# Writing out every engine's order by hand in a recurrent-attention and expert kernel

## The chip, the cores and the metric

The kernel runs on one core of a Trainium2 chip. The metric is the device time of one execution in microseconds (us), lower is better. TensorE (PE) multiplies matrices, VectorE (DVE), ScalarE (ACT) and GpSimd (POOL) work elementwise, and SyncE (SP) issues the DMA transfers. Each engine works through its own list of instructions in the order in which the program lays it down, and instructions of different engines wait for each other by semaphores.

## The reference

Two stages follow each other. The first is a linear attention with decay, over 4 batches, 8 heads, 768 steps and a head size of 48; the second is a dense layer pair with an unusual activation on the resulting 3072 tokens of width 384.

```python
for t in range(S):
    kt, vt, rt = (k[:, :, t], v[:, :, t], r[:, :, t])
    cur = np.einsum('bhd,bhe->bhde', u[None] * kt, vt)
    y[:, :, t] = np.einsum('bhd,bhde->bhe', rt, state + cur)
    state = w[None, :, :, None] * state + np.einsum('bhd,bhe->bhde', kt, vt)
# x: y as 3072 tokens x 384
h = x @ w_in                       # 384 -> 2048
sp = np.maximum(h, 0.0) + np.log1p(np.exp(-np.abs(h)))
g = h * erf(sp)
return (g @ w_out).astype(np.float32)   # 2048 -> 384
```

All of it is float32. w lies between 0.85 and 0.95.

## The kernel before

**Attention.** The 768 steps are cut into chunks of 128; with 4 batches there are 24 chunks g, four of which (one of each batch) make one block of 512 tokens. Within a chunk the recurrence becomes matrix products, for which r and k are scaled by powers of w. A chunk passes through named steps: L loads it, K and R scale k and r (L180, L184, 112 x 512 each), N scales the k that lies the other way round (L188, 128 x 384), Q forms the diagonal: two multiplies (L200, L201), a sum (L202) and two spread-out halves `am` (L211 on ScalarE as four small multiplies, or L213 on GpSimd as one large). A is the product of k and r on TensorE (L232), whose masked part is copied over `am` (L239); Y multiplies by v and adds the part of the carried state `sbd` (L256); S forms the state's increment `ds` (L279) and updates `sbd` (L289 to L292); X splits the result into a high and a low half (L301, L302), for the next stage.

**Expert layers.** Float32 accuracy comes from pairs of numbers: each operand is a high half that TensorE takes at full rate and the remainder, and three products stand for one. A step n is one block b of 512 tokens and one of 16 slices f of the 2048 columns, 96 steps in all; the first two blocks are worked through in halves of eight slices, with partial sums kept in DRAM. `f1` makes h with nine matmuls (L319). The activation is a chain of ScalarE and VectorE instructions of 128 x 512: two tanh (L326, L327), a combination (L329), tanh and two squares (L335 to L337), a product with h (L342), the high half `gh` (L348) and the remainder `gl` (L354, on VectorE or GpSimd). `f2` adds nine matmuls into three accumulators (L371). There are three buffers for h, two for each tile of the chain.

**Weights.** They come as 64-bit words, in 16 groups of 768 columns, and are turned into the high and low halves on the chip: L114 (ScalarE), L115, L116, L118 (VectorE), L120 (ScalarE, the high half) and L121 (VectorE or GpSimd, the low half). Group 0 of `win` is needed for f 0 and 1, and so on; all 16 groups are turned while the first two blocks run.

**Order.** A table `PLAN` gives each step of a chunk and of a weight group a place on the scale of the step number n, `FFN` gives the distances of the pieces of one step, and the program emits all pieces sorted by that place. The framework's own scheduler then orders the instructions anew within each engine, from its estimates of their durations. Three tables, `ONDVE`, `ONACT` and `GLP`, and `SUBDVE` for the weights, say which engine takes which elementwise piece. TensorE is given some matmuls on zeros (`keep_warm`, L85) where it would stand idle early on.

```python
for n in range(NS):
    for d, f in zip(FFN, (f1, act_a, act_b, act_c, act_d, act_e, f2)):
        todo.append((n + d - (0.95 if f is f1 and n == NS - 1 else 0), f, (n,)))
for (what, *args), pos in PLAN.items():
    todo.append((pos, parts[what], args[:1] if what == "W" else args))
todo.sort(key=lambda x: x[0])
```

A second path under `tc.If` serves values of w that the fast path can't take; it doesn't run with these inputs.

Of the kernel before, what the change touches and what calls it, by code (L numbers as in the profile page):

```python
# [9 lines left out]
F32 = mybir.dt.float32  # L10
# [30 lines left out]
def body(ctx: ExitStack, tc: tile.TileContext, att, wcol, u, win, wout, levels, outT):  # L41
# [20 lines left out]
    def load_chunk(g, parts=((0, V0), (V0, AW))):  # L62
        if g >= NCH:
            return
        if g not in chunks:
            chunks[g] = (xp if g == 3 else apool).tile([P, AW], F32, tag="x" if g == 3 else "att", name=f"att{g}")
        for c0, c1 in parts:
            nc.sync.dma_start(out=chunks[g][:, c0:c1], in_=att[g, :, c0:c1])
# [33 lines left out]
    def load_w(which, g):
        if (which, g) not in raws:
            fetch_w(which, g)
        raw = raws.pop((which, g))
# [4 lines left out]
        words = raw.bitcast(I32).rearrange("p (n two) -> p n two", two=2)  # L110
        wl, wh = words[:, :, 0], words[:, :, 1]
        t = stage.tile([P, WG], I32, tag="wt", name=f"wt{which}{g}", bufs=WTB)
        v = t.bitcast(F32)
        nc.scalar.activation(out=v, in_=wh.bitcast(F32), func=AF.Copy, scale=2.0 ** -112)  # L114
        nc.vector.tensor_scalar(out=t, in0=t, scalar1=3, scalar2=None, op0=ALU.logical_shift_left)  # L115
        nc.vector.scalar_tensor_tensor(out=t, in0=wl, scalar=29, in1=t,  # L116
                                       op0=ALU.logical_shift_right, op1=ALU.bitwise_or)
        nc.vector.scalar_tensor_tensor(out=t, in0=wh, scalar=-0x80000000, in1=t,  # L118
                                       op0=ALU.bitwise_and, op1=ALU.bitwise_or)
        nc.scalar.copy(out=hi, in_=v)  # L120
        (nc.vector if (which, g) in SUBDVE else nc.gpsimd).tensor_tensor(out=lo, in0=v, in1=hi.bitcast(F32), op=ALU.subtract)  # L121
# [56 lines left out]
    def prep_k(g):  # L178
        t = chunks[g][:PR, 512:V0]
        pick("k", g).tensor_tensor(out=t, in0=t, in1=wk.rearrange("p a c -> p (a c)"), op=ALU.mult)  # L180

    def prep_r(g):
        t = chunks[g][:PR, 0:512]
        pick("r", g).tensor_tensor(out=t, in0=t, in1=wr.rearrange("p a c -> p (a c)"), op=ALU.mult)  # L184

    def prep_n(g):
        t = chunks[g][:, K0:R0]
        pick("n", g).tensor_tensor(out=t, in0=t, in1=wknf, op=ALU.mult)  # L188

    def prep_q(g):  # L190
        st_[g] = dict(t=chunks[g], am=diagonal(chunks[g], g))

    def pick(what, g):
        return nc.vector if what in ONDVE.get(g, "") else nc.gpsimd

    def diagonal(t, g):

        q = a2.tile([P, NPAIR, 2], F32, tag="q", name=f"q{g}")
        kn, rn = t[:, K0:R0], t[:, R0:AW]
        pick("q", g).tensor_tensor(out=rn, in0=rn, in1=ub, op=ALU.mult)  # L200
        pick("q", g).tensor_tensor(out=rn, in0=rn, in1=kn, op=ALU.mult)  # L201
# [16 lines left out]
    def a_step(g):  # L218
# [15 lines left out]
        for hh in range(2):  # L234
            predicated(s["am"][hh], ap[hh], mask.bitcast(U32), hh)
# [356 lines left out]
```

## Time and profile before

| | |
|---|---|
| time, median of 3 runs | 572.49 us (570.76 to 576.68) |
| time of the profiled execution | 572.33 us |
| its span, first to last instruction | 570.2 us |
| busy: PE, DVE, ACT, POOL | 536.0, 338.7, 392.2, 268.7 us |
| mean granted TensorE clock | 0.968 |

In the rows below, a group reads: line, engine, operation, output <- inputs, shapes, count | busy us, mean ns of one | idle time just before them and who ended it. In a timeline the first number is the start in us, the second the length. A digit of the slices is the busy share in tenths of one fortieth of the span. Matmuls are pipelined, so the lengths of neighbours overlap; from one start to the next is the better measure.

### The profile page before, as it was taken

What the parts mean: (1) busy time and instruction counts of PE and PEld (TensorE: products, weight loads), DVE (VectorE), ACT (ScalarE), POOL (GpSimd) and SP (SyncE); (2) the same over time, 40 slices, a digit from 0 to 9 for tenths busy, and PEclk for the clock granted to TensorE, in tenths of its full rate; (3) what the DMA queues carried; (4) which work ended last, traced back from release to release, by engine and by line L of the source; (5) the groups of instructions that cost most, each with busy time, mean ns of one, the idle gap of its engine ahead of it and who ended that gap; (6) DMA issues with size and microseconds to landing.
All of it is one profiled execution on the core that took longest, in us unless ns stands there. A gap on an engine that the chain in (4) does not pass through costs nothing.

```text
span 570.2 us, 10334 instructions
## 1 busy us (share of the span) xinstructions
PE 536.0 (94%) x4107; PEld 405.1 (71%) x4107; DVE 338.7 (59%) x533; ACT 392.2 (69%) x701; POOL 268.7 (47%) x242
## 2 busy tenths in 40 slices
PE   7848988898999999999999999999999999999994
PEld 3526766675766777777777777777777778888882
DVE  8798877988657576573744345546642333445342
ACT  2424836568998946776768784776696668888783
POOL 6994489984363366474473128835412412000000
PEclk9776997999999999999999999999999999999999
DMA  7652434344243052233220014202210000010002
GB/s 290 241 214 77 172 138 143 130 137 167 64 142 109 1 174 101 82 119 118 82 83 0 2 57 162 81 1 82 82 56 1 2 1 1 0 57 0 1 0 60
DMA packets 20773, 48.89 MB, mean 86 GB/s; under 512 B 1648, under 2 KB 10992, under 8 KB 20720
## 3 DMA queue, kind: packets, MB, share of 16 engines
q1 hardware_dynamic: 20720, 48.18, 25.0%
q8 instruction: 34, 0.56, 0.4%
q14 instruction: 19, 0.16, 0.1%
HBM read 41.88 MB, written 6.29 MB: 84 GB/s over the span
## 4 chain that ended last, share of the span: by engine, by line
PE 69%; DVE 13%; ACT 6%; POOL 4%; issue 3%; DMA 2%; DVEq 0%; POOLq 0%; ACTq 0%
PE h L319 30%; PE acc L371 29%; PE y L256 5%; PE A L232 4%; DVE wt L118 2%; DVE wt L116 1%; DVE gl L354 1%; PE ds L279 1%; DVE s L329 1%; DVE s L342 1%; DVE wt L115 1%; DVE am L239 1%; ACT gh L348 1%; POOL am L213 1%; ACT wt L114 1%
## 5 line engine op out<-in xcount | busy, mean ns | idle before, releaser
L319 PE MATMUL h<-x,wih 128*128 128x512 f32 x576 | 191.8, 410 | 8.1 <-DVE s L342 4.4
L354 POOL TENSOR_TENSOR gl<-s,gh 128x512 fp32r<-128x512 f32 x49 | 64.2, 1313 | 155.8 <-ACT gh L348 150.3
L319 PEld LDWEIGHTS h<-x,wih 128*128 128x128 f32 x576 | 108.2, 193 | 39.0 <-DVE s L342 6.9
L319 PE MATMUL h<-x,wil 128*128 128x512 f32 x288 | 116.8, 406 | 0.0
L371 PE MATMUL acc<-gl,woh 128*128 128x512 f32 x288 | 115.5, 401 | 1.4 <-POOL gl L354 0.9
L342 DVE SCALAR_TENSOR_TENSOR s<-s,h 128x512 f32<-128x512 f32 x96 | 65.7, 685 | 83.1 <-ACT s L337 82.7
L371 PE MATMUL acc<-gh,wol 128*128 128x512 f32 x288 | 113.7, 395 | 0.0
L329 DVE SCALAR_TENSOR_TENSOR s<-s,h 128x512 f32<-128x512 f32 x96 | 65.7, 684 | 62.2 <-ACT s L327 52.5
L371 PE MATMUL acc<-gh,woh 128*128 128x512 f32 x288 | 96.6, 403 | 0.5 <-ACT gh L348 0.5
L335 ACT ACTIVATE s<-s 128x512 f32<-128x512 f32 x96 | 60.4, 629 | 48.0 <-DVE s L329 47.9
L348 ACT CAST gh<-s 128x512 fp32r<-128x512 f32 x96 | 59.0, 615 | 33.3 <-DVE s L342 26.0
L326 ACT ACTIVATE s<-h 128x512 f32<-128x512 f32 x96 | 57.1, 595 | 31.1 <-PE h L319 30.1
L319 PEld LDWEIGHTS h<-x,wil 128*128 128x128 f32 x288 | 55.3, 192 | 14.6 <-issue 0.8
L371 PEld LDWEIGHTS acc<-gl,woh 128*128 128x128 f32 x288 | 54.1, 188 | 16.1 <-issue 1.6
L371 PEld LDWEIGHTS acc<-gh,woh 128*128 128x128 f32 x288 | 53.3, 188 | 16.2 <-issue 2.2
L371 PEld LDWEIGHTS acc<-gh,wol 128*128 128x128 f32 x288 | 54.1, 188 | 12.0
L336 ACT ACTIVATE s<-s 128x512 f32<-128x512 f32 x96 | 60.4, 629 | 1.8
L337 ACT ACTIVATE s<-s 128x512 f32<-128x512 f32 x96 | 60.3, 629 | 1.5
L327 ACT ACTIVATE s<-s 128x512 f32<-128x512 f32 x96 | 60.3, 628 | 1.3
L213 POOL TENSOR_TENSOR am<-ident,q 128x512 f32<-128x512 f32 x37 | 43.0, 1182 | 38.5 <-PE y L256 30.8
L354 DVE TENSOR_TENSOR gl<-s,gh 128x512 fp32r<-128x512 f32 x47 | 40.1, 856 | 18.9 <-ACT gh L348 18.1
L239 DVE COPY_PREDICATED am<-mask,A 64x256 f32<-64x256 uint32 x96 | 40.1, 443 | 17.3 <-PE A L232 13.5
(72 smaller groups left out, 579.8 us busy)
## 6 DMA issues: line engine op xcount, KB each, us to landing
att<-in_att_dram SPq DMA_DIRECT2D x24, 608.0 KB, 5.0
att<-in_att_dram SPq DMA_DIRECT2D x24, 512.0 KB, 3.7
raw<-in_win_dram SPq DMA_DIRECT2D x8, 768.0 KB, 4.3
raw<-in_wout_dram SPq DMA_DIRECT2D x8, 768.0 KB, 4.4
out_dram<-o SPq DMA_DIRECT2D x18, 256.0 KB, 2.6
part<-o SPq DMA_DIRECT2D x6, 256.0 KB, 3.7
o<-part SPq DMA_DIRECT2D x6, 256.0 KB, 2.8
ub<-in_u_dram SPq DMA_DIRECT2D x1, 192.0 KB, 6.0
```

The source lines that it names most:

```text
L213: nc.gpsimd.tensor_tensor(out=m, in0=ident[:, hh:hh + 1].to_broadcast([P, NPAIR, C]), in1=q[:, :, hh:hh + 1].to_broadcast([P, NPAIR, C]), ...
L319: nc.tensor.matmul(out=h, lhsT=w[:, f, q, :], rhs=x[:, xi, q, :], start=k == 0, stop=k == 8)
L326: nc.scalar.activation(out=s1, in_=e["h"], func=AF.Tanh, bias=FB0, scale=FA0)
L327: nc.scalar.activation(out=s1, in_=s1, func=AF.Tanh, bias=FB1, scale=FA1)
L329: nc.vector.scalar_tensor_tensor(out=s2, in0=s1, scalar=FG, in1=e["h"], op0=ALU.mult, op1=ALU.add)
L335: nc.scalar.activation(out=s, in_=s, func=AF.Tanh, bias=FB2, scale=FA2)
L336: nc.scalar.activation(out=s, in_=s, func=AF.Square, bias=FB3, scale=FA3)
L337: nc.scalar.activation(out=s, in_=s, func=AF.Square, bias=FB4, scale=FA4)
L342: nc.vector.scalar_tensor_tensor(out=g, in0=g, scalar=FC, in1=e["h"], op0=ALU.subtract, op1=ALU.mult, reverse0=True)
L348: nc.scalar.copy(out=gh, in_=e["g"])
L354: (nc.gpsimd if GLPOOL(n) else nc.vector).tensor_tensor(out=gl, in0=e["g"], in1=e["gh"].bitcast(F32), op=ALU.subtract)
L371: nc.tensor.matmul(out=acc[e], lhsT=w[:, f, es], rhs=g, start=first and i == 0, stop=last and i == 2)
```

## The change

`PLAN`, `FFN` and the four tables of engines are gone. In their place stands one string, `ORDER`, of 1710 words, each one instruction or one block of instructions; the program emits them in just this sequence, inside `tc.manual_schedule()`, so that each engine's list is the sequence of its words. For that the steps are cut finer: the activation into a, b, z, c, d, e, g, h, l, the weights into C..a to C..f, the diagonal into Qa, Qb, Qc and M, the masked copies into P, the state into D and Sa to Sd, the split into Xa and Xb, the loads into their two halves, the outputs into Oa to Oc. f is `f1`, p is `f2`. A "+" at the end of a word puts it on GpSimd, a "*" on ScalarE, else VectorE or the engine that the step always has. The arithmetic of a step is as before.

| elementwise pieces on GpSimd | before | after |
|---|---|---|
| K, R (112 x 512) | 17, 18 of 24 | 8, 8 |
| N, Qa, Qb (128 x 384) | 20, 23, 23 of 24 | 5, 10, 7 |
| halves of `am` | 37 of 48 | 17 (17 on ScalarE, 14 on VectorE) |
| state times w^128 | 32 of 32 | 21 |
| low halves of the weights | 9 of 16 | 5 |
| `gl` | 49 of 96 | 43 |

`keep_warm` asks for 84 matmuls on zeros in all (16 ahead of the words, 68 by words), 37 before.

```diff
+    fixed = ctx.enter_context(ExitStack())
+    fixed.enter_context(tc.manual_schedule())
...
-    load_chunk(0, ((0, V0),))
-    load_chunk(1, ((0, V0),))
     ub = const.tile([P, 384], F32, name="ub")
-    nc.sync.dma_start(out=ub, in_=u.partition_broadcast(P))
+
+    def load_u():
+        nc.sync.dma_start(out=ub, in_=u.partition_broadcast(P))
...
+    def load_w(part, eng, which, g):
...
+        if part == "a":
+            nc.scalar.activation(out=v, in_=wh.bitcast(F32), func=AF.Copy, scale=2.0 ** -112)
+        elif part == "b":
+            nc.vector.tensor_scalar(out=t, in0=t, scalar1=3, scalar2=None, op0=ALU.logical_shift_left)
...
+        else:
+            eng.tensor_tensor(out=lo, in0=v, in1=hi.bitcast(F32), op=ALU.subtract)
...
+    def prep_k(g, eng):
         t = chunks[g][:PR, 512:V0]
-        pick("k", g).tensor_tensor(out=t, in0=t, in1=wk.rearrange("p a c -> p (a c)"), op=ALU.mult)
+        eng.tensor_tensor(out=t, in0=t, in1=wk.rearrange("p a c -> p (a c)"), op=ALU.mult)
...
+    def diag_m(q, g, hh, eng):
...
+        if eng is nc.scalar:
+            for p in range(NPAIR):
+                nc.scalar.mul(out=m[:, p, :], in_=ident[:, hh], mul=q[:, p, hh:hh + 1])
+        else:
+            eng.tensor_tensor(out=m, in0=ident[:, hh:hh + 1].to_broadcast([P, NPAIR, C]),
+                              in1=q[:, :, hh:hh + 1].to_broadcast([P, NPAIR, C]), op=ALU.mult)
...
-    for n in range(NS):
-        for d, f in zip(FFN, (f1, act_a, act_b, act_c, act_d, act_e, f2)):
-
-            todo.append((n + d - (0.95 if f is f1 and n == NS - 1 else 0), f, (n,)))
...
+    words = ORDER.split()
+    last = max(i for i, x in enumerate(words) if x[0] == "C")
+    for i, x in enumerate(words):
+        eng = {"+": nc.gpsimd, "*": nc.scalar}.get(x[-1], nc.vector)
+        what, x = x[0], x.rstrip("+*")
+        num = int("".join(c for c in x if c.isdigit()))
+        sub = x[-1]
+        if what == "l":
+            act_l(num, eng)
+        elif what in steps:
+            steps[what](num)
...
+    fixed.close()
...
-WARM = (21, 4)
...
+WARM = 16
 WG, RAWB, WTB = 768, 2, 1
...
+ORDER = """
+U0 L0a L0b L1a L1b Q0a+ L2a K0 L3a T0 R0 Q0b A0 F00 Q1a Q0c R1+ M01* F10 M00 N0 P00 R2+ W8 D0 P01 L2b C00a K2+ S0a W3
+Y0 S0b L3b Q1b A2 X0a K1 N1 A1 L4a Q1c K3+ X0b M10* D1 L4b S1b Q2a+ S1a M11* P10 Q3a+ P11 Q2b+ W10 Y1 K4 Q4a X1a L5a
...
+O230b h25 O230c l25+ f24 O232b O232c f26 a24 O231a b24 z24 c24 D9 f27 a26 S9a L11a S9b S9c+ d24 O231b b26 S9d L14a e24
...
+p71 d73 c74 e73 d74 g73 Y21 a75 e74 b75 g74 p72 X21a X21b Y22 h74 h73 l74+ f77 X22a l73 X22b z75 p73 c75 a77 d75 b77
...
+O950a O950b O951a O952a O951b O952b
+"""
```

More of the change, by code (lines that the diff above doesn't have):

```diff
@@ L98, in fetch_w @@
     def fetch_w(which, g):
-        raw = raws[which, g] = stage.tile([P, WG], I64, tag="raw", name=f"raw{which}{g}")
+        raws[which, g] = raw = stage.tile([P, WG], I64, tag="raw", name=f"raw{which}{g}")
         nc.sync.dma_start(out=raw, in_=(wout if which else win)[:, g * WG:(g + 1) * WG])
[L102 to L105, printed above, removed]
+    bits = {}
+    def load_w(part, eng, which, g):
+        words = raws[which, g].bitcast(I32).rearrange("p (n two) -> p n two", two=2)
+        wl, wh = words[:, :, 0], words[:, :, 1]
+        if part == "a":
+            bits[which, g] = stage.tile([P, WG], I32, tag="wt", name=f"wt{which}{g}", bufs=WTB)
+        t = bits[which, g]
+        v = t.bitcast(F32)
         hi, lo = (woh, wol) if which else (wih, wil)
@@ L109, in load_w @@
         hi, lo = hi.rearrange(pat)[:, s], lo.rearrange(pat)[:, s]
[L110 to L121, printed above, removed]
+        if part == "a":
+            nc.scalar.activation(out=v, in_=wh.bitcast(F32), func=AF.Copy, scale=2.0 ** -112)
+        elif part == "b":
+            nc.vector.tensor_scalar(out=t, in0=t, scalar1=3, scalar2=None, op0=ALU.logical_shift_left)
+        elif part == "c":
+            nc.vector.scalar_tensor_tensor(out=t, in0=wl, scalar=29, in1=t,
+                                           op0=ALU.logical_shift_right, op1=ALU.bitwise_or)
+        elif part == "d":
+            nc.vector.scalar_tensor_tensor(out=t, in0=wh, scalar=-0x80000000, in1=t,
+                                           op0=ALU.bitwise_and, op1=ALU.bitwise_or)
+        elif part == "e":
+            nc.scalar.copy(out=hi, in_=v)
+        else:
+            eng.tensor_tensor(out=lo, in0=v, in1=hi.bitcast(F32), op=ALU.subtract)
     ident = const.tile([P, 2, P], F32, name="ident")
@@ L372, in f2, with put_out, end @@
                                  start=first and i == 0, stop=last and i == 2)
-        if not last:
-            return
-        for e in range(NQ):
-            o = fp.tile([P, TB], F32, tag="s1" if n == NS - 1 and e == 2 else "o", name=f"o{n}_{e}")
-            if f < NF - 1:
-                nc.scalar.copy(out=o, in_=acc[e])
-                pt = part[b, e] = dp.tile([P, TB], F32, tag=f"part{b}{e}", name=f"part{b}{e}")
-                nc.sync.dma_start(out=pt, in_=o)
-                continue
+    def put_out(n, e, cols=None):
+        b = order[n][0]
+        nc.sync.dma_start(out=outT[e * P:(e + 1) * P, :, cols if cols is not None else slice(b * C, (b + 1) * C)],
+                          in_=outs[n, e].rearrange("p (s c) -> p s c", c=C))
+    outs = {}
+    def end(step, n, e):
+        b, f = order[n]
+        if step == "a":
+            o = outs[n, e] = fp.tile([P, TB], F32, tag="s1" if n == NS - 1 and e == 2 else "o", name=f"o{n}_{e}")
             if (b, e) in part:
                 nc.sync.dma_start(out=o, in_=part[b, e])
-                nc.vector.tensor_tensor(out=o, in0=o, in1=acc[e], op=ALU.add)
             elif b == NB - 1 and e > 0:
@@ L527, in GLPOOL @@
-def GLPOOL(n):
-    return n in GLP
+                for what in "fabzcdegh":
+                    steps[what](n)
+                act_l(n, nc.vector)
+                f2(n)
+            for e in range(NQ):
+                end("a", NS + NF - 1, e)
+                put_out(NS + NF - 1, e, bass.ds(blk * C, C))
+WARM = 16
+WG, RAWB, WTB = 768, 2, 1
+ORDER = """
+U0 L0a L0b L1a L1b Q0a+ L2a K0 L3a T0 R0 Q0b A0 F00 Q1a Q0c R1+ M01* F10 M00 N0 P00 R2+ W8 D0 P01 L2b C00a K2+ S0a W3
+Y0 S0b L3b Q1b A2 X0a K1 N1 A1 L4a Q1c K3+ X0b M10* D1 L4b S1b Q2a+ S1a M11* P10 Q3a+ P11 Q2b+ W10 Y1 K4 Q4a X1a L5a
```

305 lines of the change are left out of this document (189 added, 116 removed).

## The prediction

> **What bounds it now.** I read the page first (busy shares, slices, chain), then the engine table by stage, then the matmuls of each stage, and last the groups of VectorE and GpSimd instructions in the early stage.
>
> ```profile
> span 570.2 us, 10334 instructions
> PE 536.0 (94%) x4107; PEld 405.1 (71%) x4107; DVE 338.7 (59%) x533; ACT 392.2 (69%) x701; POOL 268.7 (47%) x242
> ...
> DVE  8798877988657576573744345546642333445342
> ...
> POOL 6994489984363366474473128835412412000000
> PEclk9776997999999999999999999999999999999999
> ...
> PE 69%; DVE 13%; ACT 6%; POOL 4%; issue 3%; DMA 2%; DVEq 0%; POOLq 0%; ACTq 0%
> ```
>
> By its average TensorE is 94% busy and nothing else matters. The slices say otherwise: VectorE and GpSimd are full in the first ten and thin out afterwards, and the chain spends 23% of the span on the three elementwise engines. So I cut the span at four places: the first matmul of the expert layer, 200 us, the last matmul, the end. Columns: window, length, then busy us (and instructions) of PE, PEld, DVE, ACT, POOL, the clock, the DMA share and rate.
>
> ```profile
> 0.00:46.30 46.30, 32.92 (x396) 20.49 (x396) 40.10 (x74) 14.50 (x35) 37.75 (x42) 0.80 0.64 231
> 46.30:200.00 153.70, 141.15 (x1004) 105.14 (x1007) 117.95 (x154) 112.77 (x199) 94.58 (x74) 0.95 0.36 118
> 200.00:562.40 362.40, 361.93 (x2717) 279.46 (x2709) 180.24 (x305) 264.15 (x466) 136.40 (x126) 1.00 0.16 53
> 562.40:570.20 7.80, 0.00 (x1) 0.00 (x0) 0.42 (x1) 0.75 (x2) 0.00 (x0) 0.83 0.37 107
> ```
>
> How much of the big matmuls lies behind 200 us (tiles h, acc and A, TensorE alone):
>
> ```profile
> 0.00:200.00 200.00, 66.84 (x234) 0.91 0.42 144
> 200.00:570.20 370.20, 166.87 (x630) 1.00 0.17 54
> ...
> 200.00:570.20 370.20, 171.63 (x657) 1.00 0.17 54
> ...
> 200.00:570.20 370.20, 22.86 (x448) 1.00 0.17 54
> ```
>
> And what they cost when nothing waits: two rows of the chain (start, us, what) and rows of the timeline.
>
> ```profile
> 228.88 1.67 PE y L256 x56
> ...
> 513.49 4.20 PE acc L371 x18
> ```
>
> ```profile
> 10.02 1.09 PE L232 MATMUL A<-att 48*64 48x128 f32 x32
> ...
> 203.79 1.08 PE L232 MATMUL A<-att 48*64 48x128 f32 x16
> ...
> 230.48 0.56 PE L279 MATMUL ds<-att 128*48 128x48 f32 x16
> 230.98 0.50 PE L319 MATMUL h<-x,wil 128*128 128x512 f32 x1
> ...
> 231.77 0.39 PE L319 MATMUL h<-x,wil 128*128 128x512 f32 x1
> ```
>
> Eighteen large matmuls in 4.20 us are 2.10 us for the nine of one f or p step, far below the 0.4 us that a single record shows, because records overlap. Behind 200 us stand 630 + 657 = 1287 of them, 143 steps or 300 us, in 362 us of full TensorE. Before 200 us stand 441, only 103 us of work in 200 us. So the first 200 us are not bound by TensorE; the last 362 nearly are.
>
> What binds the first 200 us is seen in the groups of that window (line, engine, tile, count, busy us, mean ns):
>
> ```profile
> L118 DVE SCALAR_TENSOR_TENSOR wt<-raw,wt 128x768 int32<-128x768 int32 x16 | 23.8, 1488 | 0.3
> L116 DVE SCALAR_TENSOR_TENSOR wt<-raw,wt 128x768 int32<-128x768 int32 x16 | 20.4, 1277 | 0.2
> ...
> L115 DVE TENSOR_SCALAR wt<-wt 128x768 int32<-128x768 int32 x16 | 16.3, 1018 | 3.8 <-ACT wt L114 3.7
> L354 DVE TENSOR_TENSOR gl<-s,gh 128x512 fp32r<-128x512 f32 x9 | 11.1, 1239 | 1.3 <-ACT gh L348 1.3
> ...
> L121 DVE TENSOR_TENSOR wil<-wt,wih 128x768 fp32r<-128x768 f32 x4 | 7.0, 1740 | 0.6 <-ACT wih L120 0.6
> ...
> L121 DVE TENSOR_TENSOR wol<-wt,woh 128x768 fp32r<-128x768 f32 x3 | 4.7, 1566 | 1.2 <-ACT woh L120 1.2
> ```
>
> The same instructions while GpSimd is idle, and one of them while GpSimd runs four multiplies in a row:
>
> ```profile
> 183.60 0.56 DVE L115 TENSOR_SCALAR wt<-wt 128x768 int32<-128x768 int32 x1 [0.58 <-ACT wt L114]
> ...
> 184.73 0.95 DVE L116 SCALAR_TENSOR_TENSOR wt<-raw,wt 128x768 int32<-128x768 int32 x1
> 185.71 0.96 DVE L118 SCALAR_TENSOR_TENSOR wt<-raw,wt 128x768 int32<-128x768 int32 x1
> 186.59 0.69 DVE L354 TENSOR_TENSOR gl<-s,gh 128x512 fp32r<-128x512 f32 x1
> ```
>
> ```profile
> 108.75 4.59 DVE L118 SCALAR_TENSOR_TENSOR wt<-raw,wt 128x768 int32<-128x768 int32 x1
> ```
>
> ```profile
> 109.32 1.27 POOL L180 TENSOR_TENSOR att<-att,wk 112x512 f32<-112x512 f32 x1
> ...
> 111.53 1.00 POOL L200 TENSOR_TENSOR att<-att,ub 128x384 f32<-128x384 f32 x1
> ```
>
> An instruction that takes 0.96 us alone took 4.59 us beside GpSimd. Mean less free time, times count: L118 16 x 0.53 = 8.4, L116 16 x 0.33 = 5.2, L115 16 x 0.46 = 7.3, L354 9 x 0.55 = 4.9, L121 4 x 0.78 + 3 x 0.61 = 4.9 (free as L118). That is 30.7 us in which VectorE counts as busy and only waits for GpSimd. The bound of the first part is these two engines getting in each other's way.
>
> **The change, stage by stage.** In the new order the word f24 stands behind 25 f and 24 p steps with ten A, so 71 + 72 = 143 steps and 14 A follow it: the cut at 200 us of the old trace. I call what lies ahead of it the first part and count words.
>
> First part, GpSimd. The old trace has 37.75 + 94.58 = 132.3 us in 116 instructions there, 102 of them multiplies and subtractions. The new order has 44: 3 K, 3 R, 2 N, 4 and 2 of Q, 8 M, 8 of S, 5 of C, 9 l. At the old mean, 44 x 132.3 / 102 = 57 us at the most. What goes to ScalarE is two halves of M more than its seven there, eight small multiplies; it was busy 14.50 + 112.77 of 200 us and has room. If that room were gone they would cost 8 x 0.39 = 3 us:
>
> ```profile
> L211 ACT ACTIVATE am<-ident,q 128x128 f32<-128x128 f32 x44 | 13.9, 389 | 9.6 <-DVE q L202 9.2 <-PE y L256 0.4
> ```
>
> First part, VectorE. It gains, against the old trace, K +5, R +5, M +5 and l +7 of 512 columns, N +8 and Q +16 of 384, the low halves of the weights +4, S +2. Two more rows (whole run) price the shorter ones:
>
> ```profile
> L188 DVE TENSOR_TENSOR att<-att,wkn 128x384 f32<-128x384 f32 x4 | 2.2, 548 | 0.0
> ```
>
> ```profile
> L291 DVE TENSOR_TENSOR sbd<-sbd,ds 48x192 f32<-48x192 f32 x32 | 11.2, 350 | 3.9 <-PE ds L279 2.0 <-PE y L256 1.3
> ```
>
> So 22 x 0.69 + 24 x 0.55 + 4 x 0.96 + 2 x 0.35 = 32.9 us. M on VectorE has no row; it reads and writes as much as L354, hence 0.69, and the dearer end is GpSimd's own price for it (below), 3.3 us more for five. The 52 instructions overlap the next by 0.08 us (186.59 starts before 185.71 + 0.96), which takes 4 off. VectorE's own work becomes (40.10 + 117.95) - 30.7 + 32.9 - 4 = 156 us.
>
> ```profile
> L213 POOL TENSOR_TENSOR am<-ident,q 128x512 f32<-128x512 f32 x15 | 20.0, 1350 | 7.0 <-DVE q L202 7.0
> ```
>
> Then the waiting on GpSimd. It was 30.7 us per 132.3 us of GpSimd; for 57 us that is 13. If it also grows with VectorE's two-operand work (16 x 2.47 + 7 x 0.96 + 9 x 0.69 = 52 us, now 85), it is 21. I take 13, because the multiplies L180 and L184 that stay contended in the 158 us are not taken out of it.
>
> The Trainium skill ("SBUF — State Buffer", section on the two separate sides) says that a VectorE instruction with two SBUF inputs and a GpSimd instruction exclude each other, and that whichever starts first holds the pair for its whole length. By that a wait ends with the GpSimd instruction in progress, 1.3 us at the most here; the row of 4.59 us went past several, so the trace agrees on the exclusion and not on the length. With 123 such VectorE instructions, a GpSimd busy 30% of the time and half of 1.3 us each, its sum would be 24 us in place of 13.
>
> Last, VectorE's idle time. The old first part has 200 - 158 = 42 us. The new order is dense in VectorE work, so I look at the densest stretch of the old one:
>
> ```profile
> 60.00:80.00 20.00, 17.96 (x233) 13.73 (x223) 18.48 (x29) 12.90 (x22) 12.91 (x12) 1.00 0.47 158
> ```
>
> 1.52 of 20 us idle is 7.6%, 14 us over the part; the ends are 6 (what the first 46 us show) and 42. First part: 156 + 13 + 14 = 183 us, instead of 200.
>
> What else lies there: TensorE's 49 steps (103 us), ten A, ten Y, nine D and 84 warming matmuls (37 before, 0.3 us each at the most, so up to 14 us more) come to some 150 us even so, under 183; they cost nothing unless TensorE becomes the bound, and then 14 us. At the old clocks (0.80 and 0.95) the 150 would be some 165, still under. The load of u (128 x 384 floats, 0.2 MB) goes first on SP's queue and the first two weight loads (128 x 768 words of 8 bytes, 0.8 MB each) ahead of the second halves of chunks 2 and 3. At the 231 GB/s of the first stage chunk 0 comes 1 us later and chunk 3 7 us; VectorE sets up powers of w meanwhile, and chunk 3 is needed last. Fixed order means that a VectorE instruction whose input is late holds every one behind it; in the first part that includes the weight halves that the next f waits for. That is the 14 us.
>
> Second part. The old 362.4 us hold 300 us of steps, 14 A, 14 or 15 Y, 10 D. The old order cuts A into pieces: one half took 1.08 us, where a whole A took 1.09 undivided, and each return to a large matmul costs 0.11 us (0.50 against 0.39). The new order writes A, Y, D, f and p as whole blocks: 143 x 2.10 + 14 x 1.09 + 14 x 1.67 + 11 x 0.56 + 39 returns x 0.11 = 349.4 us, and TensorE is the bound there (VectorE 180 us and ScalarE 264 us of 362 before, each with some 30 us more at the most). With the end of 7.8 us unchanged: 357.2.
>
> Sum: 183 + 357 = 540 us of span, and the profiled run took 572.33 us for a span of 570.2, so 542 us. Its time is 0.16 us under the median of the runs shown, so nothing is corrected.
>
> **The rivals.** (a) The two engines were the real bound of the first part, by taking turns: VectorE's 52 us of two-operand work and GpSimd's 132 make 184 of 200 us; the change makes them 85 + 57 = 142. If the waiting then vanishes, the first part is 156 + 6 = 162 us and the time 521. For it: the 4.59 us row. Against: 142 of 162 leaves little room not to meet. The page of the Trainium skill named above points here too, since exclusion between these two is the only contention it allows among the engines.
>
> (b) The first part stays at 200 because a chain of waits through ScalarE and TensorE, not VectorE's load, sets its pace (the chain has 6% ScalarE). Then only the second part gains: 200 + 357 + 2 = 559.
>
> (c) Slower: VectorE becomes the bound and keeps the idle time it has. Its queue then holds 156 + 21 + 42 us and 3 for the dearer M, 222 us, and the time is 222 + 357 + 2 = 581. It costs time from a first part of 213 us on, when waiting and idling exceed 57 us. For it: the 42 us came about under an order made by a planner too. Against: a third of them lie behind 160 us (40 - 26.04), where ScalarE is busy 90% and sets the pace.
>
> ```profile
> 160.00:200.00 40.00, 37.86 (x189) 28.27 (x191) 26.04 (x35) 35.86 (x64) 15.72 (x11) 1.00 0.23 73
> ```
>
> (d) The order isn't kept as written, or the engines run into the same waits in another place: 572.
>
> **Numbers.** Forecast 0.63, (a) 0.12, (b) 0.10, (c) 0.10, (d) 0.05. The forecast's own range: waits 13 to 21, idle 6 to 26, second part up to 6 us longer, 532 to 564. The range to hold it 8 times in 10 is 526 to 567: it leaves out (c), (d) and half of (a). About 1% is what a measurement of this kernel can tell, so faster means under 566.8: forecast, (a) and (b), less the forecast's upper edge, 0.83; within 1%: (d) and that edge, 0.07; slower 0.10.
>
> **What would show it.** Right: GpSimd about 55 us busy before the step f24, L118's mean near 1.1 us, f24 starting near 183 us, and about 350 us from there to the last matmul with A groups of 32. VectorE idle by more than 40 us before f24 speaks for (b) or (c); GpSimd waits gone and f24 before 170 us for (a). Wrong altogether: a TensorE idle in the second part, where I allow none, or a clock row below full there.

## The result, and the profile after

The changed kernel takes 550.47 us (median of 4 runs, 546.98 to 554.57), the kernel before 572.37 us beside it: a ratio of 0.961, 95% interval 0.954 to 0.969. The forecast was 542 us with a range of 526 to 567, and faster; the time lies inside, 8.5 us above the middle. The profiled run of the changed kernel took 546.98 us for a span of 545.3 us.

The page of the changed kernel: busy time by engine, VectorE, GpSimd and the clock in slices, and the shares of the chain.

```profile
span 545.3 us, 10413 instructions
PE 515.9 (95%) x4154; PEld 395.7 (73%) x4154; DVE 371.1 (68%) x631; ACT 391.0 (72%) x725; POOL 158.9 (29%) x138
...
DVE  5799999999796595596455338869649643433442
...
POOL 4644433421212132371011125514024111031100
PEclk9799988999999999999999999999999999999998
...
PE 65%; DVE 22%; ACT 5%; issue 4%; DMA 3%; SPq 0%; DVEq 0%; ACTq 0%
```

GpSimd has gone from 268.7 to 158.9 us, and VectorE is now at nine tenths or more in eight slices running, where it had two such slices, apart from each other. GpSimd has left the chain, VectorE's share of it rose from 13% to 22%.

The stages, cut at the first h matmul, at the word f24 (after 441 large matmuls, as in the prediction), the last matmul and the end. The columns are window, length, and busy us (instructions) of PE, PEld, DVE, ACT, POOL, then clock, DMA share and rate.

```profile
0.00:38.90 38.90, 30.50 (x417) 17.70 (x417) 29.86 (x79) 16.16 (x42) 19.49 (x26) 0.91 0.75 260
38.90:180.40 141.50, 133.45 (x1044) 102.11 (x1043) 129.86 (x203) 114.28 (x199) 45.66 (x33) 0.98 0.37 125
180.40:538.40 358.00, 351.94 (x2696) 275.89 (x2694) 210.93 (x349) 260.05 (x483) 93.70 (x81) 1.00 0.17 57
538.40:545.30 6.90, 0.00 (x0) 0.00 (x0) 0.42 (x1) 0.50 (x2) 0.00 (x0) 0.69 0.43 122
```

The same cut of the kernel before, at its own f24, which stands at 201.0 us:

```profile
46.30:201.00 154.70, 142.15 (x1034) 105.98 (x1033) 118.65 (x156) 113.59 (x200) 94.89 (x75) 0.95 0.35 117
201.00:562.40 361.40, 360.93 (x2682) 278.62 (x2679) 179.55 (x304) 263.33 (x464) 136.10 (x126) 1.00 0.16 53
```

So of 24.9 us of span the first part gave 201.0 - 180.4 = 20.6, the second 361.4 - 358.0 = 3.4, the end 0.9.

VectorE's groups of the first part of the changed kernel (line, engine, tiles, count, busy us, mean ns, idle before them). L122, L125, L120, L370 and L130 are the old L116, L118, L115, L354 and L121.

```profile
L122 DVE SCALAR_TENSOR_TENSOR wt<-raw,wt 128x768 int32<-128x768 int32 x16 | 15.5, 968 | 0.1
L125 DVE SCALAR_TENSOR_TENSOR wt<-raw,wt 128x768 int32<-128x768 int32 x16 | 15.2, 949 | 0.1
L370 DVE TENSOR_TENSOR gl<-s,gh 128x512 fp32r<-128x512 f32 x16 | 12.2, 770 | 1.5 <-ACT gh L365 1.4
L120 DVE TENSOR_SCALAR wt<-wt 128x768 int32<-128x768 int32 x16 | 10.2, 638 | 1.1 <-ACT wt L118 1.0
L130 DVE TENSOR_TENSOR wol<-wt,woh 128x768 fp32r<-128x768 f32 x6 | 6.3, 1050 | 1.0 <-ACT woh L128 0.9
```

The two costliest groups are at the price that they have alone: 0.97 and 0.95 us where they were 1.28 and 1.49.

Below, **waiting** of VectorE means the sum, over its instructions in a part, of their length less the shortest length of the same operation at the same line and with as many columns in that run; **own** is busy less waiting, **idle** the length of the part less busy. **Stalls** are gaps of TensorE in the second part: after a large matmul, the time to the next start less 0.23 us, summed where it is over 0.15 us and not the 0.1 us that an entry into or a return from the attention matmuls costs; a gap behind an attention matmul isn't in that sum.

### The profile page after: what moved, and what is told of

The parts are those of the page before. It is cut to its first block, busy times and chain, and to the rows that moved or that the text cites. A ratio compares the mean times of both kernels' runs of the same rounds, so it can differ in the third digit from the quotient of the medians.

```text
span 545.3 us, 10413 instructions
## 1 busy us (share of the span) xinstructions
PE 515.9 (95%) x4154; PEld 395.7 (73%) x4154; DVE 371.1 (68%) x631; ACT 391.0 (72%) x725; POOL 158.9 (29%) x138
## 4 chain that ended last, share of the span: by engine, by line
PE 65%; DVE 22%; ACT 5%; issue 4%; DMA 3%; SPq 0%; DVEq 0%; ACTq 0%
PE acc L386 28%; PE h L327 28%; PE y L261 5%; DMA att<-in_att_dram 3%; DVE am L244 3%; PE A L238 2%; DVE att L193 2%; DVE s L343 2%; DVE gl L370 2%; DVE att L201 2%; DVE att L189 1%; DVE s L359 1%; DVE wt L122 1%; DVE wt L125 1%; DVE att L197 1%
## 5 line engine op out<-in xcount | busy, mean ns | idle before, releaser
L327 PE MATMUL h<-x,wih 128*128 128x512 f32 x576 | 184.6, 402 | 1.7 <-DVE s L359 1.6
L327 PEld LDWEIGHTS h<-x,wih 128*128 128x128 f32 x576 | 106.7, 189 | 30.0 <-DVE s L359 3.5
L370 POOL TENSOR_TENSOR gl<-s,gh 128x512 fp32r<-128x512 f32 x43 | 60.6, 1413 | 210.0 <-ACT gh L365 201.5
L386 PE MATMUL acc<-gh,woh 128*128 128x512 f32 x288 | 115.7, 402 | 0.4 <-ACT gh L365 0.4
L327 PE MATMUL h<-x,wil 128*128 128x512 f32 x288 | 114.6, 398 | 0.0
L359 DVE SCALAR_TENSOR_TENSOR s<-s,h 128x512 f32<-128x512 f32 x96 | 64.8, 683 | 66.3 <-ACT s L355 66.1
L343 DVE SCALAR_TENSOR_TENSOR s<-s,h 128x512 f32<-128x512 f32 x96 | 65.2, 682 | 46.3 <-ACT s L338 41.8
L370 DVE TENSOR_TENSOR gl<-s,gh 128x512 fp32r<-128x512 f32 x53 | 40.6, 769 | 18.4 <-ACT gh L365 17.7
L238 PE MATMUL A<-att 48*64 48x64 f32 (+1 forms) x768 | 27.8, 262 | 5.5 <-DVE sbd L294 1.9
```

Of the source, the lines that this page charges most:

```text
L327: nc.tensor.matmul(out=h, lhsT=w[:, f, q, :], rhs=x[:, xi, q, :], start=k == 0, stop=k == 8)
L343: nc.vector.scalar_tensor_tensor(out=e["s"], in0=e["s1"], scalar=FG, in1=e["h"], op0=ALU.mult, op1=ALU.add)
L359: nc.vector.scalar_tensor_tensor(out=s, in0=s, scalar=FC, in1=ff[n]["h"], op0=ALU.subtract, op1=ALU.mult, reverse0=True)
L370: eng.tensor_tensor(out=e["gl"], in0=e["s"], in1=e["gh"].bitcast(F32), op=ALU.subtract)
L386: nc.tensor.matmul(out=acc[e], lhsT=w[:, f, es], rhs=g, start=first and i == 0, stop=last and i == 2)
```

## The experiments

One table of all kernels run. The ratio is to the kernel before, measured beside it on the same chip; before took 572.4 us (4 runs), 572.3 (13), 572.3 (7), 572.4 (11) and 572.7 (7). The parts are those of each kernel's profiled run.

| kernel | us, median (runs) | ratio, 95% interval | first part | second part |
|---|---|---|---|---|
| before | 572.4 | | 201.0 | 361.4 |
| changed | 550.5 (4) | 0.961 [0.954, 0.969] | 180.4 | 358.0 |
| changed, again | 550.4 (4) | 0.961 [0.954, 0.967] | 183.5 | 359.5 |
| new order, old engines | 580.6 (4) | 1.017 [1.009, 1.024] | 201.7 | 370.2 |
| old order, new engines | 568.4 (10) | 0.994 [0.991, 0.997] | 199.2 | 359.8 |
| new words, scheduler free | 586.4 (4) | 1.025 [1.018, 1.032] | 204.6 | 373.3 |
| without the 68 warming matmuls | 551.8 (4) | 0.964 [0.958, 0.971] | 185.2 | 358.6 |
| nothing on GpSimd | 553.5 (4) | 0.968 [0.964, 0.971] | 188.8 | 357.9 |
| A by halves | 554.0 (4) | 0.969 [0.962, 0.975] | 184.6 | 360.8 |
| second-part preparation off GpSimd | 546.1 (4), 549.0 (6) | 0.955 [0.951, 0.959], 0.958 [0.954, 0.962] | 181.0, 183.0 | 356.9, 357.4 |
| and four words earlier | 550.4 (5) | 0.959 [0.954, 0.964] | 181.6 | 358.1 |
| and dense places relieved | 545.7 (4) | 0.952 [0.949, 0.955] | 183.0 | 355.8 |
| both of these | 548.1 (4) | 0.958 [0.957, 0.960] | 178.9 | 359.3 |

My theory at the start was that of the prediction: GpSimd's smaller share is what frees the first part, through less waiting. Its first rival was that the sequence alone does it. "New order" in the table means all that the change does except the choice of engines: the sequence, its being binding, the finer steps, the earlier loads and the warming matmuls. No run has an order written by hand for the old engines, so what that would be worth stays open.

### The new order on the old engines

The marks of 175 words are set so that each piece goes to the engine that the old tables gave it; the sequence stays.

```diff
-U0 L0a L0b L1a L1b Q0a+ L2a K0 L3a T0 R0 Q0b A0 F00 Q1a Q0c R1+ M01* F10 M00 N0 P00 R2+ W8
+U0 L0a L0b L1a L1b Q0a+ L2a K0+ L3a T0 R0 Q0b+ A0 F00 Q1a+ Q0c R1 M01* F10 M00* N0+ P00 R2 W8
...
```

> The new order, word for word, but each elementwise piece on the engine that the old tables gave it (175 words change their mark). Theory 1, that GpSimd standing in VectorE's way set the old first part: GpSimd is again about 130 us busy ahead of f24, VectorE waits about 30 us for it instead of 12, f24 starts near 198 us and not 180, the time is about 567. Rival, the sequence alone made the gain: f24 stays within 5 us of 180 and the time within 6 us of 550.

Measured: 580.6 us, slower than before. Stages from its first h to f24 and from there to the last matmul, and the three waits of its first part that bear on it (engine, line <- whom it waits for: us, times, longest):

```profile
45.00:201.70 156.70, 138.61 (x1042) 104.06 (x1043) 121.62 (x161) 114.77 (x199) 95.23 (x74) 0.96 0.33 109
201.70:571.90 370.20, 353.50 (x2696) 277.12 (x2695) 191.29 (x303) 255.57 (x467) 139.04 (x131) 1.00 0.16 55
```

```profile
DVE s L359 <- ACT s L355: 11.2, 10, 2.1
...
DVE q L208 <- POOL att L204: 6.7, 2, 3.6
...
PE A L238 <- POOL att L193: 3.3, 1, 3.3
```

And TensorE's longest stop in the second part, VectorE's row first:

```profile
451.50 0.55 DVE L208 TENSOR_REDUCE q<-att 128x8 f32<-128x384 f32 x1 [5.45 <-POOL att L204]
...
452.70 0.73 PE L327 MATMUL h<-x,wih 128*128 128x512 f32 x2 [3.51 <-DVE s L359]
```

An order written for other engines keeps nothing of the gain in the first part and loses 12 us in the second, where TensorE is idle for 370.2 - 353.5 = 16.7 us. In a fixed list everything stands behind an instruction that comes late: here VectorE's sum waits 5.45 us for GpSimd, the activation's product stands behind it in VectorE's list, and TensorE waits 3.51 us for that. The rival falls. My theory held for the first part (198 us forecast, 201.7 measured; VectorE waits 32.1 us) and not for the time, 567 us: it had no loss in the second part.

### The old order on the new engines

The kernel before with its tables filled from the words of the new one (Qa, Qb, the halves of `am` and the state products get tables of their own).

```diff
-        pick("q", g).tensor_tensor(out=rn, in0=rn, in1=ub, op=ALU.mult)
-        pick("q", g).tensor_tensor(out=rn, in0=rn, in1=kn, op=ALU.mult)
+        pick("a", g).tensor_tensor(out=rn, in0=rn, in1=ub, op=ALU.mult)
+        pick("b", g).tensor_tensor(out=rn, in0=rn, in1=kn, op=ALU.mult)
...
-SUBDVE = ((0, 0), (0, 1), (0, 4), (0, 6), (1, 0), (1, 1), (1, 2))
+SUBDVE = ((0, 1), (0, 3), (0, 4), (0, 6), (0, 7), (1, 0), (1, 1), (1, 2), (1, 3), (1, 5), (1, 6))
```

> The old planner with its old places, but each elementwise piece on the engine that the new words give it. Theory 1: VectorE's waiting falls from 31 to about 13 us, the cut of 50 steps comes at about 187 us and not 200, the second part stays at 362, the time is about 558. Rival, the sequence alone made the gain: 572 or more, since the places were chosen for the old engines and VectorE has 33 us more to do ahead of the cut.

Measured: 568.4 us, 0.6% faster than before. The same two stages, and the row of `gl` in the first part:

```profile
40.60:199.20 158.60, 142.83 (x1036) 106.30 (x1034) 136.62 (x204) 115.13 (x202) 48.84 (x37) 0.92 0.35 118
199.20:559.00 359.80, 359.79 (x2682) 279.16 (x2679) 199.37 (x347) 266.11 (x480) 88.00 (x77) 1.00 0.16 53
```

```profile
L354 DVE TENSOR_TENSOR gl<-s,gh 128x512 fp32r<-128x512 f32 x17 | 16.3, 960 | 5.1 <-ACT gh L348 5.0
```

The mean of `gl`, 0.96 us, lies between the 1.24 us of the kernel before and the 0.77 us of the changed one. The first h comes 5.7 us earlier than before, at 40.6 us, and that is lost again by f24. So my theory falls too, as the only cause: the same split of the work is worth 1.8 us of the first part under the old order and 20.6 under the new one. What VectorE's first part is made of, in us:

| kernel | own | waiting | idle | sum | GpSimd busy |
|---|---|---|---|---|---|
| before | 121 | 37.6 | 42.2 | 201.0 | 132.6 |
| new order, old engines | 121 | 32.1 | 48.9 | 201.7 | 126.0 |
| old order, new engines | 149 | 23.6 | 26.9 | 199.2 | 68.4 |
| changed | 147 | 13.0 | 20.7 | 180.4 | 65.2 |

Moving the work gives VectorE 28 us more to do and takes 14 us of waiting and 15 of idling away: hardly anything is left over. Only the order that goes with this split halves the waiting once more, at the same GpSimd load (68.4 and 65.2 us), and takes another 6 us of idling.

### The new words with the scheduler free

```diff
-    fixed.enter_context(tc.manual_schedule())
```

> The new words, without the line that fixes the order, so the framework's scheduler may move instructions. If the order is worth something as written: the A blocks are cut again (16 in place of 32, 6 us in the second part), first part 185 to 190, time 556 to 565. If the emission order and the engines are all that counts: 550 within 4 us. If the scheduler hides the words altogether: 565 to 575.

Measured: 586.4 us, the slowest kernel of all. Its second part, and the A matmuls in that part (the same windows, tile A on TensorE alone), first of this kernel and then of the changed one:

```profile
204.60:577.90 373.30, 371.39 (x2696) 285.31 (x2694) 203.94 (x351) 261.78 (x482) 92.92 (x81) 1.00 0.16 52
...
204.60:577.90 373.30, 28.08 (x448) 1.00 0.16 52
```

```profile
180.40:538.40 358.00, 15.27 (x448) 1.00 0.17 57
```

The scheduler cuts A into pieces again, 28.1 us in place of 15.3, and VectorE's first part has 39.2 us idle. No expectation of mine reached as far as 586. The sequence alone, as a suggestion, is worth less than the old planner's; that it is binding is part of the gain.

### The warming matmuls

All ten W words are taken out, so 68 of the 84 dummy matmuls go.

```diff
-... P00 R2+ W8 D0 P01 L2b C00a K2+ S0a W3 Y0 S0b
+... P00 R2+ D0 P01 L2b C00a K2+ S0a Y0 S0b
```

> All ten words that put matmuls on zeros into TensorE's list are left out (84 become 16); nothing that is computed changes. Theory 1, VectorE sets the pace of the first part: f24 within 3 us of 180, time within 4 us of 550. Rival, a warmer TensorE made part of the gain: the granted clock of the first 180 us falls from 0.96 to 0.85 or less, h and A steps there take up to twice as long, f24 comes 6 to 12 us later and the time is 556 to 562.

```profile
PEclk9687878999999999999999998999999999999998
```

The granted clock over the first part is 0.90, where the two profiles of the changed kernel have 0.96 and 0.95, so it didn't fall as far as the rival asked. The time is 551.8 us beside 550.4 for the unaltered one, no difference that can be measured, though f24 stands at 185.2 us, outside the 3 us that I allowed and 1.7 us behind the later of those profiles. A TensorE slower by this much costs nothing in the first part that these runs can tell.

### The changed kernel once more

> The changed kernel once more, unaltered, beside the three below on one chip: 547 to 553 by every theory, with f24 near 182 us and some 357 us from there to the last matmul.

Measured: 550.4 us; f24 at 183.5, second part 359.5 us. The parts of one kernel differ by 2 to 3 us between profiles, and differences of that size in the table say nothing.

### GpSimd in the second part

The second part was to take 349 us and took 358. The trace of the changed kernel shows what looked like the cause: VectorE and GpSimd in the largest stall (start, length, instruction, idle time before).

```profile
330.90 4.05 DVE L193 TENSOR_TENSOR att<-att,wr 112x512 f32<-112x512 f32 x1
334.87 0.68 DVE L370 TENSOR_TENSOR gl<-s,gh 128x512 fp32r<-128x512 f32 x1
...
330.89 1.28 POOL L193 TENSOR_TENSOR att<-att,wr 112x512 f32<-112x512 f32 x1
332.13 1.01 POOL L201 TENSOR_TENSOR att<-att,ub 128x384 f32<-128x384 f32 x1
333.11 1.28 POOL L189 TENSOR_TENSOR att<-att,wk 112x512 f32<-112x512 f32 x1
...
335.60 0.50 PE L386 MATMUL acc<-gl,woh 128*128 128x512 f32 x1 [1.27 <-DVE gl L370]
```

A VectorE multiply of 0.7 us is held for 4.05 us until three GpSimd instructions in a row are through; the remainder `gl` behind it comes late, and TensorE stands. So 33 words K, R, N, Q, M behind f24 go from GpSimd to VectorE:

```diff
-z26 A10 a27 g24 L11b c26 f29 P100 h24 b27 l24 O231c d26 R11 L14b e26 K14+ z27 p24 a29 P101 c27 R14+ g26 b29 d27 f28
+z26 A10 a27 g24 L11b c26 f29 P100 h24 b27 l24 O231c d26 R11 L14b e26 K14 z27 p24 a29 P101 c27 R14 g26 b29 d27 f28
...
```

> From f24 on the 33 words K, R, N, Q and M that stood on GpSimd go to VectorE; S and the remainders l stay. Theory 2, the second part is 8 us over its matmuls because VectorE's list is held up behind GpSimd and gl comes late: VectorE's waiting in the second part falls from 23 to 10 us or less, the stalls in f2 vanish, the second part is 351 to 354 us instead of 358, the time 544 to 547. Rival, those stalls come from VectorE's queue being long, whoever holds it: 33 pieces more in it, about 20 us, make the second part 360 or longer, the time 552 or more.

Measured: 546.1 us, and VectorE's waiting in the second part falls from 23.0 to 8.8 us as expected. But the second part takes 356.9 us, not 351 to 354. And with nothing at all on GpSimd (the "+" of 124 words removed):

> Every word that stood on GpSimd (124) goes to VectorE, same order. Theory 1: VectorE waits no more for GpSimd (12 us less in the first part), and works 24 us more there, so f24 comes at 190 to 194 us; the second part loses its stalls and comes to 352 to 355; the time is 550 to 556. If blocking were the whole of it, below 545; if VectorE can't carry the load in the order given, 565 or more.

```profile
40.00:188.80 148.80, 136.92 (x1043) 103.95 (x1044) 139.44 (x236) 114.22 (x199) 0.00 (x0) 0.95 0.35 116
188.80:546.70 357.90, 351.60 (x2696) 275.98 (x2694) 235.97 (x430) 259.61 (x483) 0.00 (x0) 1.00 0.17 57
```

Measured: 553.5 us; the first part is 5 to 8 us longer than in the two profiles of the changed kernel, and the second part is 357.9 us with GpSimd empty, as long as with 94 us on it. GpSimd made that one stall, which is gone in both kernels; it doesn't make the stalls' sum, 6.8 us with nothing on it.

### Four words earlier, and VectorE relieved

In the kernel without second-part preparation on GpSimd the largest stalls stand at three places (1.1 us more stand at p94, near the end), and at each of the three a word that TensorE waits for has preparation ahead of it in VectorE's list. Four words are moved (the lines show the places alone; g69 goes ahead of Q22b, and not of P201 as the expectation says):

```diff
-... e26 K14 z27 p24 a29 P101 c27 R14 g26 ...
+... e26 g26 K14 z27 p24 a29 P101 c27 R14 ...
-... h34 S14d P120 Q13a f39 h35 P121 Q13b l34 p34 ...
+... h34 l34 S14d P120 Q13a f39 h35 P121 Q13b p34 ...
-... e69 Q21b d70 Q22b b72 p68 Q21c N21 e70 g69 M211 Q22c h69 g70 f71 ...
+... e69 Q21b g69 d70 Q22b b72 p68 Q21c e70 g70 N21 M211 Q22c h69 f71 ...
```

> The kernel without second-part preparation on GpSimd (e6), with four words of VectorE's list moved ahead of preparation that nothing waits for yet: g26 ahead of K14, z27, P101 and R14; l34 ahead of P120, Q13a, P121 and Q13b; g69 ahead of P201 and Q22b's follow-up, g70 ahead of N21. Theory (what is left of TensorE's idle time in the second part is the place of g and l in VectorE's list, and not GpSimd): the stalls of 1.33, 1.49 and 0.91 us at those three places go, 3.7 us in all; the second part takes about 353 us instead of 356.9, the time 542.5 us instead of 546.1. Rival (VectorE's work is simply too dense at these places, so that a word moved ahead delays another one that TensorE needs as soon): the stalls come back a few us later, the second part stays at 356 us or more and the time at 545.5 or more.

> The kernel without second-part preparation on GpSimd once more, unaltered, beside the one with four words moved, on the same chip: 546 us (545 to 547), stalls again about 6 us, the largest at the same words (h27 after the step 26, l34, f71). Rival (the place of the stalls changes from run to run): other places, and the difference between the two kernels says nothing about the words.

Measured: 550.4 us, beside 549.0 for the kernel without the move. That kernel has its stalls at the same words as in its first profile (1.11, 1.49 and 0.95 us), so they are no accident of a run. With the words moved they come back a few us later, at the next word of the same stretch: 2.40 us ahead of step 35's `gl` and 1.92 us ahead of A22, and at the first place 0.56 us at an A and 0.57 at a Y. The windows of the stretches ahead of the three stalls in the unmoved kernel, then its whole second part and a stretch in which TensorE has no stall:

```profile
186.00:197.50 11.50, 9.60 (x81) 6.96 (x79) 8.77 (x17) 9.10 (x17) 0.50 (x1) 1.00 0.79 266
240.00:250.40 10.40, 9.11 (x66) 6.70 (x64) 10.29 (x22) 3.98 (x9) 0.00 (x0) 1.00 0.41 138
412.00:425.70 13.70, 12.36 (x79) 9.17 (x77) 13.62 (x26) 9.81 (x20) 1.37 (x1) 1.00 0.04 15
183.00:540.40 357.40, 351.43 (x2696) 275.88 (x2694) 213.37 (x382) 260.34 (x483) 51.88 (x48) 1.00 0.17 57
334.50:353.00 18.50, 18.50 (x156) 14.58 (x155) 18.45 (x36) 14.35 (x33) 1.30 (x1) 1.00 0.11 35
```

VectorE is busy for 10.29 of 10.40 us and 13.62 of 13.70 ahead of the second and third place, 60% on average. Where it has no gap, a word that goes ahead puts another one back. My theory of the words' place falls; the new one is the amount of work in these stretches. Two of the rows already speak against it as the whole answer: ahead of the first place VectorE is busy for 8.77 of 11.50 us only, and from 334.5 to 353 us it is busy for 18.45 of 18.50 us and TensorE never stands. To test it, K14 and R14 go back to GpSimd and six halves of `am` to ScalarE:

```diff
-... K14 ... R14 ... M150 ... M151 ... M120 ... M200 ... M211 ... M220 ...
+... K14+ ... R14+ ... M150* ... M151* ... M120* ... M200* ... M211* ... M220* ...
```

> The kernel without second-part preparation on GpSimd (e6), but with VectorE relieved where its list is full: K14 and R14 back on GpSimd, and the six halves of am M120, M150, M151, M200, M211 and M220 on ScalarE. The kernel e6 showed VectorE busy for 10.29 of 10.40 us and for 13.62 of 13.70 us ahead of its stalls at the steps 34 and 71, 60% on average. Theory (TensorE's stalls in the second part come from VectorE being full for about 10 us at a time, so that neither the place of a word nor GpSimd decides, only the amount of work): 1.2 to 1.8 us less of VectorE work at each of three places takes the stalls of 1.3, 1.5 and 0.9 + 0.8 us there to 0.3 or less each; the second part takes about 353.5 us instead of 357, the time about 3.5 us less than the 546 and 549 us measured for e6. Rival (ScalarE, which takes 1.28 us for such a half and stands in order too, hands the wait on through gh or tanh): stalls of 5 us or more in sum, second part 356 us or more.

> The same relief of VectorE in the kernel with four words moved earlier (e8). Theory (VectorE being full decided, and the place of the words only once there is room): the stalls of 2.40 us at step 35 and 1.92 us at A22 shrink to 0.6 or less each, second part about 353 us, time within 1 us of the other relieved kernel. Rival (the moved words themselves make those two stalls): they stay above 1.5 us each, second part 356 us or more.

Measured: 545.7 us, the lowest median here, and 548.1 us with the words moved as well. The stalls sum to 4.3 us in the first of them (5.8 and 5.6 without the relief) and to 7.1 us in the second; the second parts, 355.8 and 359.3 us, are not the 353 to 353.5 that I expected. By place, in the first: at f28, where K14 and R14 went to GpSimd, the stall goes. At f71 it halves (0.95 to 0.47 us) and the one at A22 (0.79 us) goes, while 1.15 us appear at a Y behind them, so nothing is gained there. The one at step 34 stays, 1.40 us. The relieved kernel's stretches ahead of these two places:

```profile
238.60:249.00 10.40, 9.36 (x68) 7.03 (x66) 8.71 (x19) 7.70 (x22) 0.00 (x0) 1.00 0.42 138
411.00:424.00 13.00, 12.70 (x107) 9.57 (x108) 11.48 (x21) 11.83 (x30) 1.36 (x1) 1.00 0.01 3
```

VectorE is down from 10.29 to 8.71 of 10.40 us ahead of step 34, and the stall is as long as before. There the trace shows the rival at work, ScalarE's halves of `am` first and what waits for them:

```profile
243.46 2.46 ACT L219 ACTIVATE am<-ident,q 128x128 f32<-128x128 f32 x8 [0.62 <-DVE q L208]
...
245.95 0.77 DVE L244 COPY_PREDICATED am<-mask,A 64x256 f32<-64x256 uint32 x2 [1.56 <-ACT am L219]
...
248.46 0.69 DVE L370 TENSOR_TENSOR gl<-s,gh 128x512 fp32r<-128x512 f32 x1
...
249.20 0.50 PE L386 MATMUL acc<-gl,woh 128*128 128x512 f32 x1 [1.24 <-DVE gl L370]
```

Two halves in a row take ScalarE 2.46 us, VectorE's copy waits 1.56 us for them, and `gl` is as late as before, though ScalarE had been busy for only 3.98 of 10.40 us there in the kernel without the relief. With the words moved as well, the stall ahead of step 35's `gl` is 2.57 us, as the rival had it, and TensorE's granted clock is 0.81 from 244 to 253 us, where it is full in the rest of the part. So the relief worked at the one place where the work went to GpSimd, and gained nothing at the two where it went to ScalarE. The theory that VectorE's fullness alone makes the stalls isn't borne out; what makes the one at f71 stays open. In time the relieved kernel can't be told from the one without the relief (intervals 0.949 to 0.955 and 0.951 to 0.959). Against the changed kernel the 5 us of the relieved one are likely and not certain: the intervals of the two ratios, 0.949 to 0.955 and 0.954 to 0.967, just overlap.

### A by halves

The loop over the two row halves goes outermost in A, so that neighbouring matmuls use the same rows of the array.

```diff
-        for p in range(NPAIR):
-            for c0, i0 in ((0, 0), (H, H)):
-                for hh in range(2):
+        for hh in range(2):
+            for p in range(NPAIR):
+                for c0, i0 in ((0, 0), (H, H)):
```

> The 16 products of A are emitted with the loop over the two row halves outermost, the way the old kernel's scheduler cut them; nothing else. As I costed it, a half costs what an undivided A costs: 1.0 us more for each of 14 A in the second part, which TensorE bounds, and nothing in the first: second part 371 instead of 358, time 561 to 565. Rival, two halves overlap only by accident or the time is hidden: 550 within 3 us.

Tile A on TensorE, first and second part of this kernel:

```profile
0.00:184.60 184.60, 17.75 (x320) 0.95 0.44 150
184.60:545.40 360.80, 22.18 (x448) 1.00 0.17 56
```

The 14 A of the second part cost 22.2 us in place of 15.3, that is 0.49 us more for each. The second part is 1.3 to 2.8 us longer than in the two profiles of the changed kernel, not 6.9. The stalls sum to 3.3 us, where those profiles have 6.8 and 7.9: a longer A gives VectorE time where TensorE would have stood. Two halves one after the other cost 1.58 us, and not twice an undivided A, as I had costed them from one row. The time, 554.0 us, is at the edge of what can be told from 550.4.

## Why the prediction was right, and where it was wrong

**The direction and the split of the span**: right. The first part isn't bound by TensorE, and it ends earlier: f24 at 180.4 and 183.5 us in two profiles, where 183 stood. That it comes out so closely is partly luck, for two of the three terms were off, with opposite signs, and the third came from a sum that was too small. ("Full in the first ten" slices was too strong for GpSimd: its digits there run from 4 to 9.)

- VectorE's own work: 156 us forecast, 147 measured. The step that failed is the 30.7 us that I took out as old waiting: it summed six groups only, and all of VectorE's instructions together waited 37.6 us. Its own work before was 121 us, not 127, and the 32.9 us added less 4 bring it to 150.
- Waiting: 13 forecast, 13.0 measured (14.1 in the second profile). The size was right by luck, its rule, waiting in proportion to GpSimd's busy time, was not. From all 37.6 us of the old waiting it gives 37.6 x 65.2 / 132.6 = 18.5 us for the changed kernel, which waited 13.0, and 19.4 for the old order on the new engines, which waited 23.6. The waiting depends on the order as well as on the load.
- Idle time: 14 forecast, 20.7 measured. The densest stretch of the old trace was too good a model for the whole part.
- GpSimd: 57 us at the most was forecast, 65.2 measured, its few setup instructions with it. Its 9 `gl` alone take 16.5 us in the first part, 1.84 us each, where the shortest takes 1.29: a GpSimd instruction gets longer here too.

**The second part**: 349.4 us forecast, 358.0 measured, 8.6 us more, and this is the step that failed; the first part and the end came out 2.6 and 0.9 us under the forecast. A, Y, D, f and p run as whole blocks, as forecast (14 A groups of 32 and 15.3 us). What a block costs is seen from start to start, here around one A of the changed kernel:

```profile
203.62 0.39 PE L386 MATMUL acc<-gh,wol 128*128 128x512 f32 x1
203.94 1.09 PE L238 MATMUL A<-att 48*64 48x128 f32 x32
204.96 0.51 PE L386 MATMUL acc<-gh,woh 128*128 128x512 f32 x1
205.30 0.39 PE L386 MATMUL acc<-gl,woh 128*128 128x512 f32 x1
205.53 0.39 PE L386 MATMUL acc<-gh,wol 128*128 128x512 f32 x1
```

A large matmul takes 0.23 us to the next start (205.30 to 205.53), 0.32 where A follows it, and 0.34 where it is the first behind an A. I counted 39 returns at 0.11 us; there are 33, because a Y and a D stand next to each other six times, and the 33 cost 3.5 us and not 4.3. The 33 entries, 0.09 us each, are missing from the sum: 3.1 us. A and D, priced by lengths that overlap the next instruction, take 1.7 us less than forecast. And I allowed no stalls where there are 6.8 us of them, and 1.1 us more behind an A at f29. Together 349.4 - 0.8 + 3.1 - 1.7 + 6.8 + 1.1 = 357.9, the measured part. A TensorE idle in the second part was my own sign of being wrong altogether; it is idle there for 358.0 - 351.94 = 6.1 us.

The gap at f29 is 0.4 to 1.5 us in every profile with the new sequence in fixed order save one, that without the 68 warming matmuls, which has none; no experiment was aimed at it. In the changed kernel:

```profile
187.15 0.69 DVE L413 TENSOR_TENSOR o<-o,acc 128x512 f32<-128x512 f32 x1 [1.10 <-DMA o<-part]
...
188.86 0.68 DVE L359 SCALAR_TENSOR_TENSOR s<-s,h 128x512 f32<-128x512 f32 x1
...
189.60 0.73 PE L327 MATMUL h<-x,wih 128*128 128x512 f32 x2 [1.02 <-DVE s L359]
```

VectorE stands 1.10 us for the DMA that brings back a partial sum, the activation's product waits behind that in its list, and TensorE waits 1.02 us for the product. So TensorE's gaps have more than one cause: this DMA, GpSimd where it held VectorE for 4.05 us, K14 and R14 ahead of f28, ScalarE's halves where they were put; for the others the cause is open.

The argument that VectorE, with its 180 us and some 30 more, leaves the bound to TensorE was right in its size (210.9 us measured) and was an average over a part in which a fixed list has places where one word comes late: the mistake that the prediction avoids for TensorE at its very start. In the kernel before, TensorE had hardly a stall there (360.93 of 361.40 us busy) and spent 22.9 us on A cut into pieces in place of 15.3. So the change pays in stalls what it saves on A and on entries and returns, and keeps 3.4 us. That the scheduler's pieces of A filled just these gaps is likely, by the experiment with A by halves, and not shown.

**The rest of the difference**: 542 was for a profiled run, and the profiled run took 547.0, the fastest of its four; the median lies 3.5 us above it. The end took 6.9 us for 7.8. The forecast's own range, 532 to 564, doesn't follow from the terms named with it: added at their ends they give 534 to 568.

**The rivals.** (a), waiting that vanishes and a first part of 162 us, didn't come: 13 us of waiting stayed. (b), another chain that keeps the first part at 200 us, didn't come either. (c) and (d) didn't come either, but each is near to something that a part of the change does alone. As in (c), the new split without the new order adds 28 us to VectorE, which still waits 23.6 us and idles 26.9, and the first part stays at 199.2 us; as in (d), the new words without being binding lose the gain, and more, with 586 us. I had each of them as a mishap of the change, and neither as a sign that its parts only work together: by the medians, the order alone costs 8 us, the split alone gains 4, and both gain 22.

**The page of the Trainium skill** that I weighed ("SBUF — State Buffer", the section on the two separate sides) says that of a VectorE instruction with two inputs in SBUF and a GpSimd instruction that reads SBUF the one that starts first holds the shared ports for its whole length. From it I estimated 24 us of waiting in the first part. The changed kernel shows 13.0 us, the old order on the same engines 23.6: an estimate from chance meetings can't tell the two apart, and the order does. As to the length, the row of 4.05 us above went past three GpSimd instructions: the exclusion is borne out once more, one instruction as its longest span isn't.

## What to carry to other kernels

Dividing work among engines and ordering it are one decision: here the new order alone cost 8 us, the new split alone gained 4, and both together gained 22. When a stage is sized by an engine's average load, look for the places where its fixed list meets something late, a DMA, another engine's result or a long run of its own work: each can stop TensorE. A word moved within a full stretch moved the stall here, and work handed to an engine with room in its row handed the wait on where the result was needed soon, so read what waits for the moved work before you move it.

## What the runs showed of the hardware that was not expected

- A VectorE instruction that waits for GpSimd doesn't always get its turn when GpSimd's instruction ends: a multiply of 0.7 us was held 4.05 us over three GpSimd instructions of 1.28, 1.01 and 1.28 us.
- At nearly the same GpSimd load (68.4 and 65.2 us) VectorE waited 23.6 us under one order and 13.0 us under another.
- A change between large matmuls of 512 columns and the small ones of A, Y and D costs TensorE about 0.1 us in either direction, though neither waits: 0.32 and 0.34 us from start to start around an A, 0.23 elsewhere.
- Sixteen small matmuls of A that use one half of the rows, and then sixteen of the other, take 22.2 / 14 = 1.58 us; alternating between the halves they take 15.3 / 14 = 1.09 us.
- Taking out 68 warming matmuls lowered the granted clock of the first part to 0.90 (0.96 and 0.95 with them) and left the time where it was (551.8 and 550.4 us).
